# Moving the tiles of a gated attention-and-MLP kernel in SBUF: 512 bytes left unused low on the left, 2016 bytes at the top of the right

## The chip, the cores and the metric

The kernel runs on one core of a Trainium2 chip. The metric is the device time of one execution in microseconds (us); of a kernel that was run several times the median counts, and smaller is better. The core has five engines with a queue each: PE (TensorE, matrix products), ACT (ScalarE), DVE (VectorE), POOL (GpSimd) and SP (SyncE, which issues most DMAs). Tiles lie in SBUF, 128 partitions with the same layout of bytes in each; products land in PSUM, in banks of 512 float32 per partition. An address below is always the byte within a partition, since a tile starts at the same byte in all its partitions.

## The reference

Two branches over the same 2048 rows of x (512 columns) are mixed by a gate, one number for each row:

```python
def _A_ref(x, wqkv, wo):                 # attention, 32 heads of 16 columns
    H = 32; Dh = D // H
    q, k, v = ...                        # x @ wqkv, split in heads
    scores = jnp.einsum("bhqd,bhkd->bhqk", q, k) * Dh ** -0.5
    p = _softmax(scores, axis=-1)
    o = jnp.einsum("bhqk,bhkd->bhqd", p, v)
    return o (heads side by side) @ wo

def _B_ref(x, w1, w3, w2):               # gated MLP, inner width 1792
    h = _silu(x @ w1) * (x @ w3)
    return h @ w2

g = _sigmoid((x * gate_w).sum(-1, keepdims=True))
return g * a + (1 - g) * b
```

All inputs and the output are float32.

## The kernel before

**Products in three terms.** A float32 matrix product other than the attention's is made of three matmuls of type float32r: each operand is split into a high part and a low part (`xH`, `xL`; `fh`, `fl`), and high·high, high·low and low·high are added up in one PSUM bank. A matmul has two operands: the stationary one, up to 128 columns of 4 bytes (512 bytes of each partition), which a weight load (PEld in the profile) puts into the array first, and the moving one, here nearly always 512 columns (2048 bytes of each partition), which then streams through. In the profile's names `f<-xH,fh` the moving operand comes first and the stationary one second.

**Stages.** A prologue of some 85 us transposes x into `xH` and `xL`, computes Q and K of the first 8 heads (`project_qk`, L181) and all of V (`sums_v`, through `three`, L95 to L97). The main loop follows, written out by a string `order` of letters, and takes most of the time:

- `Q` (`score`, L719): the scores of two heads for 128 keys and 512 queries, two matmuls side by side on the upper and the lower half of the array's rows (stationary `Kt`, moving `Qt`, 50 rows each), into one of two PSUM tiles `S`; then ACT takes the exponential of it into one of ten tiles `p` (L723).
- `F` (`feed`): one matmul each of two other products, again side by side on the two halves of the rows (64 rows each). These products are the rest of Q and K and the MLP's two inner products (`w_product`, L409: stationary weights `fh`, `fl`, `raw`, `gw`; moving `xH`, `xL`), then h @ w2 (`h_product`, L518: stationary pieces of h in `fh`, `fl`, `raw`, `fr`, `gw`, `hx`; moving w2, which has taken the place of x in the tiles `xH`, `xL`), and part of the attention's last product (`o_product`, L597).
- `P` (`pv`, L706): the sums over keys p·V of two of the finished `p` tiles, in float32, four matmuls on four groups of the array's columns (stationary 17 columns of `V`, moving `p`).

A unit of the loop is eight `Q`. The first 83 units are

```python
one = "QFFF" * 7 + "QPPPP"
two = ["QFFF" * 5 + "QPPQQPP", "QFFF" * 6 + "PPQQPP"]
order = "QQFFF" + one * LONG + "".join(two[...] for i in range(short))
order += "QFFF" * 4 + "QPPQPP"
```

with LONG = 83, and with MID = 0 all of the 44 later units are `two[0]`. Counted out, the string has 2 + 127·8 + 6 = 1024 `Q` and 3 + 83·21 + 44·15 + 12 = 2418 `F`. PE executes this in the order of the string. A `Q` waits until ACT has emptied the `S` tile that was filled two `Q` earlier.

After the loop, `three` (L95 to L97) makes the last products with wo: for t = 6 and 7 with stationary pieces `ot` in `raw` and `gw`, and from t = 8 on with stationary `Oh`, `Ol`, which lie in `xH`, `xL` and `p`. The moving tiles are the same in both (`wo_`: parts of `xH3`, `xL3`, `p8`, `p9`).

**Where tiles lie.** SBUF is given out from two ends. Pools without a side stack up from low addresses: constants, then `xH`, `xL` (pool `xp`), `V` (`vp`), `Qt`, `Kt` (`qkp`), and in the loop the tiles `p` and `u` (`wk`). Pools with `side="right"` stack down from the top: `fw` (tags that begin with f: `fr`, `fh1`, `fl1`, `fh3`, `fl3`), `fk` (`gw`, `raw`, `sg`, `hx`, `gs`), and for the prologue `p1` (`xn`, `wh`, `wl`, `hi`, `lo`). In the loop the left side ended at byte 185856 and the right side began at 188384, with 2528 bytes between them. The built program gives these starts:

| tiles | side | bytes of one | start of the first | remainder by 2048 | by 512 | by 64 |
|---|---|---|---|---|---|---|
| `ident` | left | 512 | 16512 | 128 | 128 | 0 |
| `xH`, `xL` | left | 8192 | 17920 | 1536 | 0 | 0 |
| `V` | left | 34816 | 83456 | 1536 | 0 | 0 |
| `Qt` | left | 4096 | 118272 | 1536 | 0 | 0 |
| `Kt` | left | 8192 | 126464 | 1536 | 0 | 0 |
| `p`, `u` | left | 4096, 2048 | 142848 | 1536 | 0 | 0 |
| `xn`, `wh`, `wl`, `hi`, `lo` | right | 2048 to 8192 | 146016 | 608 | 96 | 32 |
| `gw`, `raw`, `sg`, `hx`, `gs`, `fr` | right | 2048 | 188384 | 2016 | 480 | 32 |
| `fh1`, `fl1`, `fh3`, `fl3` | right | 2048 | 212960 | 2016 | 480 | 32 |

Every tile of a row has the remainders of its row. A stationary slice of `xH`, `Kt`, `fh` or `raw` begins 512 bytes times a whole number behind the start of its tile, and a moving slice 2048 bytes times a whole number behind it, but for `V` in the products of L706, whose slices of 17 columns begin at any multiple of 4.

Of the kernel before, what the change touches and what calls it, by code (L numbers as in the profile page):

```python
# [8 lines left out]
F32 = mybir.dt.float32  # L9
# [8 lines left out]
P = 128  # L18
# [15 lines left out]
def gated_mix_kernel(ctx: ExitStack, tc: tile.TileContext, x, wqkv, wo, w1, w3, w2, gate_w, out):  # L34
# [20 lines left out]
    out = out[0]  # L55

    const = ctx.enter_context(tc.tile_pool(name="const", bufs=1))
    dram = ctx.enter_context(tc.tile_pool(name="dram", bufs=1, space=DRAM))
    psum = ctx.enter_context(tc.tile_pool(name="psum", bufs=1, space=PSUM))
    xp = ctx.enter_context(tc.tile_pool(name="xp", bufs=1))  # L60
    vp = ctx.enter_context(tc.tile_pool(name="vp", bufs=1))
    qkp = ctx.enter_context(tc.tile_pool(name="qkp", bufs=1))
    fw = ctx.enter_context(tc.tile_pool(name="fw", bufs=2, side="right"))
    fk = ctx.enter_context(tc.tile_pool(name="fk", bufs=2, side="right"))
    ph1 = ExitStack()
# [782 lines left out]
```

## Time and profile before

| what | value |
|---|---|
| median of three runs | 1423.19 us (1422.14 to 1423.74) |
| profiled execution, span | 1417.6 us |
| median of the runs less that span | 5.6 us |
| PE busy in the span | 1408.8 us, 99% |
| ACT busy | 1033.2 us, 73% |
| DVE, POOL busy | 449.4 us, 32%; 321.1 us, 23% |
| mean share of the DMA engines | 39.6% for the main queue |

The profile gives the span of one execution, from its first to its last instruction; the device time of the three runs is longer by 5.6 us at the median, for what lies around the span. In the timeline's rows each number in front is the start of the first instruction of a group in us, the second the time from there to the end of its last one, and "x2" the count. Ends of matmuls are modelled (one matmul overlaps the next), so the spacing of two starts says how long PE took, and the second number does not.

### The profile page before, as it was taken

To read this page: it belongs to the slowest core of one execution; us is meant where nothing else is said; L and a number is where in the kernel's file an instruction comes from. 1 tells how busy PE (TensorE), PEld (TensorE's weight loads), DVE (VectorE), ACT (ScalarE), POOL (GpSimd) and SP (SyncE) were. 2 spreads that over 40 slices of the span, in tenths; PEclk is the share of its full clock that TensorE was granted. 3 is DMA by queue.
4 is the path that set the end of the run, shared out by engine and by line. 5 is a ranking of instruction groups with operands and counts; after the bars stand their busy time and mean duration, and the time that the engine had idled before them with its cause. 6 is when DMAs were issued, how large, how long until landed. Compare 5 with 4: busy or idle time off the path is not lost.

```text
span 1417.6 us, 28518 instructions
## 1 busy us (share of the span) xinstructions
PE 1408.8 (99%) x11399; PEld 833.7 (59%) x11399; DVE 449.4 (32%) x845; ACT 1033.2 (73%) x1153; POOL 321.1 (23%) x356
## 2 busy tenths in 40 slices
PE   9999999999999999999999999999999999999998
PEld 7865656656556566565565665655555555554556
DVE  4421102464555545455464545400000000000013
ACT  4556767777777777777777777777788778877870
POOL 5014443011011100110110015441332332233230
PEclk9999999999999999999999999999999999999999
DMA  7554455342124432223233234543534443345445
GB/s 197 141 121 114 126 140 128 73 110 69 46 61 85 113 69 61 70 72 87 68 76 79 76 81 122 136 101 74 126 81 102 104 105 70 66 112 106 106 133 182
DMA packets 112668, 141.42 MB, mean 100 GB/s; under 512 B 16400, under 2 KB 70672, under 8 KB 109456
## 3 DMA queue, kind: packets, MB, share of 16 engines
q1 hardware_dynamic: 110384, 135.72, 39.6%
q10 hardware_dynamic: 2144, 3.80, 0.8%
q8 instruction: 92, 1.51, 0.5%
q14 instruction: 48, 0.39, 0.1%
HBM read 90.70 MB, written 48.76 MB: 98 GB/s over the span
## 4 chain that ended last, share of the span: by engine, by line
PE 93%; POOL 0%; DMA 0%; DVE 0%; ACT 0%; issue 0%; SPq 0%; ACTq 0%; POOLq 0%
PE acc L706 32%; PE f L409 27%; PE S L719 19%; PE f L518 11%; PE f L597 1%; PE f L95 0%; PE f L97 0%; PE f L96 0%; DMA fr<-in_B_w_dram 0%; PE S L97 0%; PE S L96 0%; PE S L95 0%; POOL xL L489 0%; POOL fl L489 0%; DVE sg L458 0%; POOL xH L488 0%
## 5 line engine op out<-in xcount | busy, mean ns | idle before, releaser
L723 ACT ACTIVATE p<-S 128x1024 f32<-128x1024 f32 x1024 | 967.5, 1026 | 308.4 <-PE S L719 307.1
L706 PE MATMUL acc<-p,V 128*17 128x512 f32 x4096 | 473.5, 594 | 0.0
L719 PE MATMUL S<-Qt,Kt 50*128 50x512 f32 x2048 | 427.9, 413 | 1.1 <-POOLq L278 0.6
L719 PEld LDWEIGHTS S<-Qt,Kt 50*128 50x128 f32 x2048 | 193.8, 184 | 187.4 <-ACT p L723 80.4
L706 PEld LDWEIGHTS acc<-p,V 128*17 128x17 f32 x4096 | 102.8, 97 | 274.1 <-issue 273.9
L409 PE MATMUL f<-xL,fh 64*128 64x512 f32 x1024 | 205.1, 391 | 0.0
L409 PE MATMUL f<-xH,fl 64*128 64x512 f32 x1024 | 204.9, 390 | 0.0
L409 PE MATMUL f<-xH,fh 64*128 64x512 f32 x1024 | 204.7, 390 | 0.0
L440 DVE RECIPROCAL sg<-sg 128x64 f32<-128x64 f32 x448 | 201.2, 509 | 1.9
L409 PEld LDWEIGHTS f<-xL,fh 64*128 64x128 f32 x1024 | 99.4, 187 | 21.2
L409 PEld LDWEIGHTS f<-xH,fl 64*128 64x128 f32 x1024 | 98.5, 185 | 20.1
L409 PEld LDWEIGHTS f<-xH,fh 64*128 64x128 f32 x1024 | 99.4, 187 | 17.7
L321 POOL CAST fh<-fr 128x512 fp32r<-128x512 f32 x32 | 21.6, 674 | 371.1 <-DMA fr<-in_B_w_dram 246.5
L687 DVE COPY u<-acc 128x512 f32<-128x512 f32 x32 | 22.1, 692 | 257.0 <-PE acc L706 257.0
L518 PE MATMUL f<-xH,fl 64*128 64x512 f32 x224 | 82.2, 391 | 0.5 <-POOL fl L489 0.5
L518 PE MATMUL f<-xL,fh 64*128 64x512 f32 x224 | 82.2, 391 | 0.3 <-POOL xL L489 0.3
L518 PE MATMUL f<-xH,fh 64*128 64x512 f32 x224 | 82.1, 391 | 0.0
L518 PE MATMUL f<-xH,raw 64*128 64x512 f32 x192 | 74.9, 390 | 0.0
L532 DVE TENSOR_SCALAR gs<-f,omg 128x512 f32<-128x512 f32 x16 | 12.0, 751 | 176.4 <-PE f L518 176.4
L432 DVE COPY gs<-f 128x512 f32<-128x512 f32 x56 | 38.7, 691 | 78.1 <-PE f L409 78.1
L518 PE MATMUL f<-xH,fr 64*128 64x512 f32 x160 | 62.4, 390 | 0.0
L454 DVE TENSOR_TENSOR raw<-f,gs 128x512 f32<-128x512 f32 x50 | 34.1, 682 | 82.7 <-PE f L409 82.7
(216 smaller groups left out, 1309.6 us busy)
## 6 DMA issues: line engine op xcount, KB each, us to landing
Kt<-kH_d SPq DMA_DIRECT2D x128, 128.0 KB
h_d<-sg SPq DMA_DIRECT2D x56, 256.0 KB
sg<-h_d SPq DMA_DIRECT2D x43, 256.0 KB
fr<-in_B_w_dram SPq DMA_DIRECT2D x42, 256.0 KB
Qt<-qH_d SPq DMA_DIRECT2D x128, 64.0 KB
Kt<-kL_d SPq DMA_DIRECT2D x64, 128.0 KB
fr<-in_A_wqkv_dram SPq DMA_DIRECT2D x18, 256.0 KB
Qt<-qL_d SPq DMA_DIRECT2D x64, 64.0 KB
```

What stands on the lines that cost most here:

```text
L321: nc.gpsimd.tensor_copy(wh, r)
L409: nc.tensor.matmul(ps, w[i == 2][r, k, :], (xL if i == 1 else xH)[b][r, k, :], start=n == 0 and r.start == 0, stop=n == 3 * ND - 1 and r.s ...
L432: nc.vector.tensor_copy(gs, ps)
L440: small.append(lambda q=q: nc.vector.reciprocal(sg[:, q:q + 64], sg[:, q:q + 64]))
L454: nc.vector.tensor_mul(gu, ps, st["gs"])
L518: nc.tensor.matmul(ps, hs[t][q][i == 2][r, P * o:P * o + P], (w2L if i == 1 else w2H)[q][r, o, :], start=n == 0 and r.start == 0, stop=n = ...
L532: nc.vector.tensor_scalar(y, ps, omg[:, t:t + 1], None, op0=OP.mult)
L597: nc.tensor.matmul(ps, ot[t][i == 2][r, P * k:P * k + P], wo_[k][i == 1][r, :], start=n == 0 and r.start == 0, stop=n == 3 * ND - 1 and r. ...
L687: nc.vector.tensor_copy(u, acc)
L706: nc.tensor.matmul(acc[r:r + DH + 1, :], V[:, k, 2 * j + h, :], p[:, h, :], start=k == 0, stop=k == NT - 1)
L719: nc.tensor.matmul(ps[:, h, :], Kt[i][r:r + 50, P * k:P * k + P], Qt[i][r:r + 50, t:t + 512], start=True, stop=True)
L723: nc.scalar.activation(p, ps, AF.Exp, scale=SCALE)
```

## The change

The change allocates two tiles that nothing writes or reads. `low_pad`, 128 float32 (512 bytes), comes right after the constants, so every left tile behind it starts 512 bytes higher. `top_pad`, 504 float32 (2016 bytes), is the first on the right, so every right tile starts 2016 bytes lower. The two together take the 2528 bytes that were free.

```diff
@@ -55,11 +55,15 @@
     const = ctx.enter_context(tc.tile_pool(name="const", bufs=1))
+    low_pad = ctx.enter_context(tc.tile_pool(name="low_pad", bufs=1))
+    low_pad.tile([P, 128], F32, name="low_pad")
     dram = ctx.enter_context(tc.tile_pool(name="dram", bufs=1, space=DRAM))
     psum = ctx.enter_context(tc.tile_pool(name="psum", bufs=1, space=PSUM))
     xp = ctx.enter_context(tc.tile_pool(name="xp", bufs=1))
     vp = ctx.enter_context(tc.tile_pool(name="vp", bufs=1))
     qkp = ctx.enter_context(tc.tile_pool(name="qkp", bufs=1))
+    top_pad = ctx.enter_context(tc.tile_pool(name="top_pad", bufs=1, side="right"))
+    top_pad.tile([P, 504], F32, name="top_pad")
     fw = ctx.enter_context(tc.tile_pool(name="fw", bufs=2, side="right"))
     fk = ctx.enter_context(tc.tile_pool(name="fk", bufs=2, side="right"))
```

The order of instructions on all five engines, and what each waits for, is the same in both built programs; only line numbers behind the change are higher by four. PSUM and DRAM addresses are the same. The starts become:

| tiles | start of the first, now | remainder by 2048 | by 512 | by 64 |
|---|---|---|---|---|
| constants with `ident` | unchanged | 128 (`ident`) | 128 | 0 |
| `xH`, `xL`, `V`, `Qt`, `Kt`, `p`, `u` | 18432 (`xH0`) | 0 | 0 | 0 |
| `xn`, `wh`, `wl`, `hi`, `lo` | 144000 | 640 | 128 | 0 |
| `gw`, `raw`, `sg`, `hx`, `gs`, `fr`, `fh`, `fl` | 186368 (`gw`) | 0 | 0 | 0 |

## The prediction

> **What bounds the kernel now.** I read the page first: busy shares, the clock, the chain of work that ended last, and the costliest groups.
>
> ```profile
> span 1417.6 us, 28518 instructions
> ...
> PE 1408.8 (99%) x11399; PEld 833.7 (59%) x11399; DVE 449.4 (32%) x845; ACT 1033.2 (73%) x1153; POOL 321.1 (23%) x356
> ...
> PEclk9999999999999999999999999999999999999999
> ...
> PE 93%; POOL 0%; DMA 0%; DVE 0%; ACT 0%; issue 0%; SPq 0%; ACTq 0%; POOLq 0%
> ...
> L723 ACT ACTIVATE p<-S 128x1024 f32<-128x1024 f32 x1024 | 967.5, 1026 | 308.4 <-PE S L719 307.1
> ...
> L409 PE MATMUL f<-xL,fh 64*128 64x512 f32 x1024 | 205.1, 391 | 0.0
> ```
>
> PE is busy 99% of the span at a granted clock near full speed, and 93% of the chain is PE's. No queue and no DMA ends a long wait, so what the change is worth is what it does to the spacing of matmuls. The change moves no instruction; only addresses differ. So the question is whether the trace shows a spacing that goes with an address. I therefore asked for PE's timeline in one unit of the main loop, with one row per letter of the order.
>
> ```profile
> 192.17 0.50 PE L719 MATMUL S<-Qt,Kt 50*128 50x512 f32 x2
> 192.51 0.40 PE L409 MATMUL f<-xH,fh 64*128 64x512 f32 x2
> ...
> 193.21 0.39 PE L719 MATMUL S<-Qt,Kt 50*128 50x512 f32 x2
> 193.45 0.39 PE L409 MATMUL f<-xH,fh 64*128 64x512 f32 x2
> 193.68 0.40 PE L409 MATMUL f<-xL,fh 64*128 64x512 f32 x2
> 193.91 0.40 PE L409 MATMUL f<-xH,fl 64*128 64x512 f32 x2
> 194.15 0.40 PE L719 MATMUL S<-Qt,Kt 50*128 50x512 f32 x2
> ...
> 198.78 0.39 PE L719 MATMUL S<-Qt,Kt 50*128 50x512 f32 x2
> 199.10 0.62 PE L706 MATMUL acc<-p,V 128*17 128x512 f32 x4
> ```
>
> From 193.21 to 198.78 six quartets QFFF take 5.57 us, 0.928 each, 0.232 per slot. No slot waits long. In all these slots the moving tile lies left, at a multiple of 512 bytes. The stationary one is `Kt` (left, multiple of 512) in a Q, and `fh` or `fl` (right, 32 bytes past a multiple of 64) in the three F.
>
> **Does a slot's time go with the address?** The products with wo after the loop answer that, since there the stationary tile goes from right to left while the moving tiles, the line of code and the shapes stay. At 1391.53 the stationary operand changes from `raw` and `gw` to `xH` and `xL`:
>
> ```profile
> 1386.17 0.39 PE L96 MATMUL f<-xL,raw 128*128 128x512 f32 x1
> ...
> 1390.83 0.39 PE L95 MATMUL f<-p,raw 128*128 128x512 f32 x1
> 1391.06 0.40 PE L96 MATMUL f<-p,raw 128*128 128x512 f32 x1
> 1391.30 0.39 PE L97 MATMUL f<-p,gw 128*128 128x512 f32 x1
> 1391.53 0.39 PE L95 MATMUL S<-xH,xH 128*128 128x512 f32 x1
> ...
> 1400.82 0.39 PE L97 MATMUL f<-xH,xL 128*128 128x512 f32 x1
> ...
> 1403.32 0.39 PE L96 MATMUL f<-p,xH 128*128 128x512 f32 x1
> ```
>
> From 1386.17 to 1391.53 there are 23 matmuls, 0.2330 each. From 1391.53 to 1403.32 there are 52, 0.2267 each. The difference is 0.0063 us, 2.7%. The output bank also changes, from `f` to `S`, but the rows from 1400.82 write `f` again and stay at 0.2267. Nor is it that the rest of the chip calms down. The busy times of both stretches (columns: PE, PEld, DVE, ACT, POOL, clock, DMA share, GB/s):
>
> ```profile
> 1386.00:1391.50 5.50, 5.50 (x24) 4.44 (x25) 1.06 (x3) 0.00 (x0) 0.00 (x0) 1.00 0.50 145
> 1391.50:1397.00 5.50, 5.50 (x26) 4.53 (x25) 1.38 (x3) 0.00 (x0) 0.00 (x0) 1.00 1.00 362
> ```
>
> The faster stretch has twice the DMA traffic and more DVE. The prologue gives two more cases: V with a right moving tile on a left stationary one, Q and K with a right stationary tile (`wh`, `wl`) lower in SBUF, at bytes that the left `p` tiles hold later.
>
> ```profile
> 83.62 0.40 PE L97 MATMUL f<-fh,xL 128*128 128x512 f32 x1
> ...
> 84.32 0.40 PE L97 MATMUL f<-fh,xL 128*128 128x512 f32 x1
> ...
> 40.00 1.09 PE L181 MATMUL S<-xH,wh 128*128 128x512 f32 x4
> ...
> 44.68 1.09 PE L181 MATMUL S<-xH,wl 128*128 128x512 f32 x4
> ```
>
> Three V matmuls take 0.70 us, 0.233 each; the twenty from 40.00 to 44.68 take 4.68, 0.234 each. So every case with one operand at 32 past a multiple of 64 stands at 0.233, wherever in SBUF it lies, and the one case with both on multiples of 512 at 0.2267. The quartet fits the same reading: one slot with both operands aligned and three with the stationary one off is 0.2267 + 3 × 0.2330 = 0.9257, against 0.928 measured. Four unaligned slots would be 0.932, four aligned ones 0.907.
>
> **The change part by part.** `top_pad` puts all the right tiles of the loop on multiples of 2048, and the prologue's on 640 past one, a multiple of 128. Whether the limit is 64, 128 or 512 bytes the trace doesn't tell; for the loop it doesn't matter. `low_pad` moves left tiles that already sit on multiples of 512. I price it at nothing: the slices of `Kt` begin at different multiples of 512 now, a new one every second Q, and the quartet shown (0.94) and the mean of six (0.928) differ by no more than the rows' rounding and the order within a pair allow.
>
> Price of an F slot. Directly, 0.2330 less 0.2267 is 0.0063. From the quartet, (0.928 − 0.907) / 3 is 0.0070. For single matmuls I take the first, for the loop the second, since it is measured there, 0.021 per quartet.
>
> Price of the P slots: none. Their moving `p` is aligned before and after, and the `V` slices stay at every multiple of 4.
>
> What limits the gain is ACT, since each quartet asks it for one exponential. The start of the loop shows ACT at its own rate, with a normal unit for comparison:
>
> ```profile
> 86.20 9.27 ACT L723 ACTIVATE p<-S 128x1024 f32<-128x1024 f32 x10 [7.85 <-PE S L719]
> ...
> 192.78 7.52 ACT L723 ACTIVATE p<-S 128x1024 f32<-128x1024 f32 x8 [2.96 <-PE S L719]
> ...
> 87.27 0.49 PE L719 MATMUL S<-Qt,Kt 50*128 50x512 f32 x2 [0.51 <-ACT p L723]
> ...
> 91.86 0.54 PE L719 MATMUL S<-Qt,Kt 50*128 50x512 f32 x2
> ...
> 88.03 1.95 ACT L723 ACTIVATE p<-S 128x1024 f32<-128x1024 f32 x2
> ...
> 90.03 0.53 PE L719 MATMUL S<-Qt,Kt 50*128 50x512 f32 x2
> ```
>
> There ACT works without a break, and PE, which waits for it, makes five quartets in 4.59 us: 0.918 each. That is what ACT sustains. Now it is asked every 0.928; after the change PE would ask every 0.907, faster than ACT can, and the backlog grows by 0.011 per quartet. The two `S` tiles give slack. In a unit the last Q starts at 198.78 and the last exponential ends at 192.78 + 7.52 = 200.30, so a tile is free 1.52 us after its Q began. The weight load of the Q that reuses it comes two quartets later less one slot: 1.814 − 0.227 = 1.587 after the change. The signal takes 0.05: in the stretch that ACT holds, the exponential that ends at 88.03 + 1.95 = 89.98 lets the Q of 90.03 go. That leaves 0.017. The unit's second Q comes 0.11 late, behind the P (192.17 to 193.21 is 1.04), so the backlog starts with the third exponential, and with the fourth it is 0.022. The Q that waits for the fourth is the sixth. So four of the unit's quartets go at 0.907 and the rest at ACT's 0.918.
>
> The sum, by places:
> - 83 long units with seven quartets: four at −0.021 and three at −0.010 are −0.114 each, −9.5 us.
> - 44 short units with five quartets: four at −0.021 and one at −0.010 are −0.094 each, −4.1 us.
> - The loop's first 3 and last 12 F, five quartets: −0.1 us.
> - The prologue has 96 matmuls of L181 and 192 with a right moving tile: 288 × 0.0063 = 1.8 us. PE has gaps there which take part of it. I take −1.0, between 0 and −1.8.
> - The 24 matmuls after the loop: −0.2 us.
>
> Together −14.9 us. The span of 1417.6 becomes 1402.7, and with the 5.6 us around it 1408.3, against the median of 1423.2. If ACT never holds PE, units give −0.147 and −0.105, with the rest −18.1: 1405.1. If it holds PE from the first quartet on, −0.070 and −0.050, with the rest −9.3: 1413.9.
>
> The P part of a unit covers what ACT still owes: its 2.96 us of idle time in the row above lie there. The one long stall in the loop is this step of the chain:
>
> ```profile
> 912.42 4.25 DMA fr<-in_B_w_dram
> ```
>
> It starts from work of PE that ends just before, and moves with it. DVE, POOL and the DMAs have idle time all along and only start earlier.
>
> **The rivals.**
> - *ACT is the bound at once* (1414). For it: 0.918 against 0.907. Against it: the slack of the two `S` tiles that I worked out. Chance 0.13.
> - *The address is not the cause* (1422 to 1423). All F slots in the trace are pairs on two halves of the rows, and no aligned pair with F's shapes is there; their 0.232 could be the price of the pair. Then only single matmuls gain, 1.2 us by the sum above, or nothing. Against it: the quartet fits one aligned and three unaligned slots within 0.002. Chance 0.11. [...]
> - *Equal offsets collide* (slower). With all large tiles on multiples of 2048, PE's two reads and the writes of ACT, POOL and DMA start at the same offset by 2048, where left and right are 480 bytes apart now. If that cost a slot what the odd start costs, 0.0063, the 2418 F would add 15.2 us: 1438.4. It decides from a mean quartet of 0.928 on. Against it: the fastest stretch, 1391.53 to 1403.32, has moving and stationary tiles at the same offset by 2048 (1536) in a quarter of its matmuls, and these are no slower in the rows, and twice the DMA traffic. Chance 0.07.
> - *More than forecast* (1403): ACT never holds PE, and Q slots, too, lose time that an F's load costs them now. A further 0.0023 per quartet (0.928 less 0.9257) would be 1.8 us over 801 quartets: 1403.3. Chance 0.05.
>
> **How the numbers follow.** The forecast, a gain of 11 to 18 us with some hold by ACT, has 0.64; the others are as above. The predicted time is 1408. The range 1403 to 1420 holds the forecast, ACT's rival and part of the last one, and leaves out the two that end at or over today's time, with 0.18 between them. A change under 0.2% (2.8 us) can hardly be told from none here. Faster by more: 0.64 + 0.13 + 0.05 = 0.82. Within it: 0.11. Slower: 0.07.
>
> **What would show it.** In the profile after, the quartet should stand near 0.907 in a unit's first half and near 0.918 at its end, the matmuls around `raw` and `gw` after the loop at 0.2267 like those behind them, V at 0.2267, and ACT's idle time before L723 (308.4 us) shorter by about what the loop gains. A quartet still at 0.928 with single matmuls at 0.2267 would mean that pairs have their own price. Quartets of 0.918 throughout would mean that ACT holds from the start. V at 0.2267 but L181 at 0.234 would say that 128 bytes are not enough. I am wrong altogether if the tail's two speeds come from something else than where a tile starts.

## The result: no gain, at most a quarter of a per cent slower

The changed kernel takes 1424.31 us (median of 22 runs, 1419.98 to 1427.12) against 1422.22 of the kernel before (22 runs, 1417.92 to 1423.74): a ratio of 1.0014, with an interval of 1.0004 to 1.0024. Predicted was 1408, with a range of 1403 to 1420. The runs of both kernels fall into two groups some 4 to 5 us apart (medians 1418.8 and 1423.2 before, 1420.4 and 1425.7 after), with about half of the runs in each, and within each group the changed kernel is the slower one, by 1.7 and by 2.5 us.

The page of the profile after, to be read against the rows of before:

```profile
span 1422.6 us, 28518 instructions
...
PE 1413.5 (99%) x11399; PEld 837.8 (59%) x11399; DVE 448.3 (32%) x845; ACT 1036.5 (73%) x1153; POOL 321.5 (23%) x356
...
PEclk9989999999999999999999999999999999999999
```

Nothing has changed in kind: PE is still busy 99%. The third digit of the clock is an 8, which was a 9. The windows of the same trace around that place (columns: length, then busy time and count of PE, PEld, DVE, ACT and POOL, then clock, DMA share and GB/s):

```profile
84.00:88.00 4.00, 3.50 (x18) 2.50 (x17) 0.00 (x0) 3.55 (x4) 0.00 (x0) 0.82 0.43 135
88.00:92.00 4.00, 4.00 (x14) 3.10 (x12) 0.00 (x0) 2.33 (x3) 0.00 (x0) 0.50 1.03 135
92.00:96.00 4.00, 4.00 (x20) 3.00 (x20) 0.00 (x0) 2.26 (x3) 0.00 (x0) 0.50 0.27 33
96.00:100.00 4.00, 4.00 (x33) 1.47 (x34) 0.00 (x0) 1.84 (x2) 0.00 (x0) 0.90 0.02 4
```

The granted clock is 0.50 from 88 to 96 us, at the start of the loop, where before's profile has 1.00. The profiled execution, 1424.69 us, is one of the upper group and has a mean granted clock of 0.996. Over a whole execution of after that mean is 0.995 to 0.996 in every run of the upper group and 0.999 to 1.000 in every run of the lower one. So the two profiled spans, after's with this dip of the clock and before's without, can't be set side by side. The trace of the kernel with the right shift alone (`top_only`, below) has no such dip (1.00 from 84 to 96 us) and a span of 1417.6 us, 5.0 less than after's. Most of the 5.0 is the dip: the unit of the loop in which it lies takes 15.15 us in after and 10.53 in `top_only`. So `top_only` is the kernel to set beside before's profile.

**The places that the prediction named.** The timeline of PE after, first at the end of the prologue (V, and the loop's first Q), then in the products with wo after the loop:

```profile
78.67 0.39 PE L101 MATMUL f<-fh,xL 128*128 128x512 f32 x1
...
82.07 0.39 PE L101 MATMUL f<-fh,xL 128*128 128x512 f32 x1
...
83.59 0.93 PE L723 MATMUL S<-Qt,Kt 50*128 50x512 f32 x4 [1.14 <-SPq L282]
```

```profile
1393.57 0.39 PE L101 MATMUL f<-p,raw 128*128 128x512 f32 x1
...
1396.51 0.39 PE L99 MATMUL S<-xH,xH 128*128 128x512 f32 x1
```

V's fifteen steps from 78.67 to 82.07 are 0.2267 each, where they were 0.233. Of the 23 with stationary `raw` and `gw`, which took 0.2330 each, the last thirteen, from 1393.57 to 1396.51, take 0.227 each; the ten ahead of them, from 1391.25 on, still take 0.231. So single matmuls did what was forecast, those behind the loop only after ten steps. Now a unit of the loop:

```profile
617.73 0.40 PE L723 MATMUL S<-Qt,Kt 50*128 50x512 f32 x2
617.96 0.40 PE L413 MATMUL f<-xH,fh 64*128 64x512 f32 x2
618.20 0.40 PE L413 MATMUL f<-xL,fh 64*128 64x512 f32 x2
618.43 0.39 PE L413 MATMUL f<-xH,fl 64*128 64x512 f32 x2
618.66 0.40 PE L723 MATMUL S<-Qt,Kt 50*128 50x512 f32 x2
...
623.33 0.39 PE L723 MATMUL S<-Qt,Kt 50*128 50x512 f32 x2
```

Six quartets QFFF take 5.60 us, 0.933 each. They took 0.928. The quartet, which should have gone to 0.907, got longer by 0.005.

**Where the time went.** The first Q and the first product with wo bound the loop. Their rows before, and then with the right shift alone:

```profile
85.33 0.93 PE L719 MATMUL S<-Qt,Kt 50*128 50x512 f32 x4 [0.61 <-POOLq L278]
...
1385.83 0.51 PE L95 MATMUL f<-xH,raw 128*128 128x512 f32 x1
```

```profile
83.67 0.93 PE L721 MATMUL S<-Qt,Kt 50*128 50x512 f32 x4 [1.20 <-SPq L280]
...
1385.89 0.50 PE L97 MATMUL f<-xH,raw 128*128 128x512 f32 x1
```

The prologue is 1.66 us shorter (85.33 to 83.67). The loop is 1.72 longer: 1385.83 − 85.33 = 1300.50 against 1385.89 − 83.67 = 1302.22. A long unit, from its first Q to the next unit's, takes 10.495 us before and 10.520 here (medians of the 83 units in the timelines). One of them, near 917 us, is no measure of the change: in before PE waits 0.28 and 0.49 us there for POOL's `xL` and `fl`, in `top_only` it doesn't, and the unit takes 11.81 and 10.80. The other 82 add 2.3 us and the 44 short ones 0.4. So the loop is 2.7 us longer apart from that wait and the prologue 1.7 shorter, which leaves 1.1, near the 1.7 that the runs show.

### The profile page after: what moved, and what is told of

It is laid out like the page before. It is cut to its first block, busy times and chain, and to the rows that moved or that the text cites. A ratio compares the mean times of both kernels' runs of the same rounds, so it can differ in the third digit from the quotient of the medians.

```text
span 1422.6 us, 28518 instructions
## 1 busy us (share of the span) xinstructions
PE 1413.5 (99%) x11399; PEld 837.8 (59%) x11399; DVE 448.3 (32%) x845; ACT 1036.5 (73%) x1153; POOL 321.5 (23%) x356
## 4 chain that ended last, share of the span: by engine, by line
PE 92%; DMA 1%; POOL 1%; issue 0%; SPq 0%; ACT 0%; DVE 0%; ACTq 0%; POOLq 0%
PE acc L710 32%; PE f L413 27%; PE S L723 19%; PE f L522 11%; PE f L601 1%; DMA fr<-in_B_w_dram 1%; POOL xL L493 0%; DMA Kt<-kH_d 0%; PE f L99 0%; PE f L100 0%; PE f L101 0%; PE S L100 0%; PE S L99 0%; PE S L101 0%; DMA fr<-h_d 0%; POOL fl L493 0%
## 5 line engine op out<-in xcount | busy, mean ns | idle before, releaser
L723 PEld LDWEIGHTS S<-Qt,Kt 50*128 50x128 f32 x2048 | 197.6, 185 | 187.8 <-ACT p L727 80.0
L413 PE MATMUL f<-xH,fh 64*128 64x512 f32 x1024 | 207.7, 396 | 0.0
L522 PE MATMUL f<-xH,fh 64*128 64x512 f32 x224 | 83.0, 395 | 0.0
```

The lines of the kernel that those rows point to most:

```text
L413: nc.tensor.matmul(ps, w[i == 2][r, k, :], (xL if i == 1 else xH)[b][r, k, :], start=n == 0 and r.start == 0, stop=n == 3 * ND - 1 and r.s ...
L522: nc.tensor.matmul(ps, hs[t][q][i == 2][r, P * o:P * o + P], (w2L if i == 1 else w2H)[q][r, o, :], start=n == 0 and r.start == 0, stop=n = ...
L723: nc.tensor.matmul(ps[:, h, :], Kt[i][r:r + 50, P * k:P * k + P], Qt[i][r:r + 50, t:t + 512], start=True, stop=True)
```

## The experiments

### One part of the change alone

Three kernels: the left shift alone (`low_only`), the right one alone (`top_only`), and the right one with 992 bytes (`top_992`), where left and right tiles are 512 apart by 2048.

```diff
 low_only:
+    low_pad = ctx.enter_context(tc.tile_pool(name="low_pad", bufs=1))
+    low_pad.tile([P, 128], F32, name="low_pad")
 top_only, and with 248 in place of 504 top_992:
+    top_pad = ctx.enter_context(tc.tile_pool(name="top_pad", bufs=1, side="right"))
+    top_pad.tile([P, 504], F32, name="top_pad")
```

> Only the 512 bytes on the left are left unused: left tiles at 0, right tiles still at 2016 past a multiple of 2048. If the pair has its own price: within 2 us of before, quartet between 0.927 and 0.934. If it is the left shift that made the loop's quartet go from 0.927 to 0.933: 3 to 5 us slower than before, since the prologue gains nothing. If equal offsets of left and right collide: as before, quartet 0.927, since the offsets still differ (by 32 bytes).

> Only the 2016 bytes on the right are left unused: left tiles at 1536, right tiles at 0 past a multiple of 2048, all on multiples of 512. If the pair has its own price: quartet 0.927 to 0.934, time within 3 us of before. If the left shift is at fault, or if equal offsets collide: quartet 0.907 to 0.918, 8 to 15 us faster than before.

> 992 bytes on the right are left unused and none on the left: left tiles at 1536, right tiles at 1024 past a multiple of 2048. Same forecast as for 2016 bytes on the right alone: a pair with its own price gives 0.927 to 0.934 per quartet; a collision of equal offsets, by 2048, gives 0.907 to 0.918; a collision of offsets equal by 1024 or 512 gives what the changed kernel has, 0.933.

Measured: `low_only` 1422.95 us, ratio 1.0004 (0.9988 to 1.0020), quartet 0.928. `top_only` 1424.60, ratio 1.0015 (1.0001 to 1.0029), quartet 0.933. `top_992` 1424.08, ratio 1.0013 (0.9998 to 1.0027), quartet 0.933. (These ratios, and those further below, are to runs of the kernel before that were made along with each of these kernels.) The left shift does nothing, the right one does all that the change does, and that left and right begin at the same offset by 2048 plays no part, since they are 512 apart in `top_only` and `top_992`. A collision of offsets that are equal by 512 would also give 0.933 in all three kernels, so these runs don't exclude it; `m1` and `q64_after` below do.

### Addresses by themselves (m1 and m3)

`m1` leaves the computation out. It has two tiles, `M` (moving) and `W` (stationary), and blocks of 48 equal matmuls, each block with its own byte offsets; its comments name them in bytes ("s" for singles, "w" for the stationary operand, "m" for the moving one). After them come pairs and quartets. One of the blocks:

```diff
+    for n in range(N):  # s w32 m0
+        nc.tensor.matmul(f[0], W[:, 8 + 128 * (n % 8):8 + 128 * (n % 8) + 128],
+                         M[:, 0 + 512 * (n % 4):0 + 512 * (n % 4) + 512], start=n == 0, stop=n == N - 1)
```

> This kernel leaves the whole computation out: it runs blocks of 48 products on one core with nothing beside them, single matmuls (128 rows) and pairs on the two halves of the rows (64 rows each), with the stationary (w) or the moving operand (m) at 0, 4, 16, 32 or 64 bytes past a multiple of 2048, and then quartets of one Q pair and three F pairs with and without an ACT exponential. Theory 'each operand off a multiple of 64 costs 0.0066 us, pairs too': singles and pairs 0.2267 at 0 and 64, 0.2333 at 32; quartets 0.907 with all at 0, 0.927 with the F weights at 32. Rival 'a pair has its own price': singles 0.2267 and 0.2333 as above, but pairs 0.232 to 0.2335 whatever the address, and quartets 0.927 to 0.934 in both. Rival 'equal offsets collide': pairs at 0 with 0 slower than pairs at 0 with 64, quartets at 0 without ACT as slow as in the loop (0.933).

The timeline has one row per block of singles. Stationary and moving offsets are, in order: 0 and 0, 32 and 0, 0 and 32, 32 and 32, 64 and 0, 16 and 0, 4 and 0:

```profile
8.05 11.15 PE L64 MATMUL f<-M,W 128*128 128x512 f32 x48
19.04 11.36 PE L67 MATMUL f<-M,W 128*128 128x512 f32 x48
30.23 11.36 PE L70 MATMUL f<-M,W 128*128 128x512 f32 x48
41.43 11.08 PE L73 MATMUL f<-M,W 128*128 128x512 f32 x48
52.35 11.36 PE L76 MATMUL f<-M,W 128*128 128x512 f32 x48
63.55 11.36 PE L79 MATMUL f<-M,W 128*128 128x512 f32 x48
74.74 11.31 PE L82 MATMUL f<-M,W 128*128 128x512 f32 x48
```

Start to start over 48, the blocks with one operand shifted stand at 0.2333 (30.23 to 41.43), also at 64 (52.35 to 63.55). The one with both at 32 is faster: 41.43 to 52.35 is 0.2275, and 0.2267 once seven or so steps have passed. So it isn't that each operand wants a multiple of 64; two equally odd starts are as good as two even ones. Pairs of 64 rows gave the same: 0.2267, 0.2333, 0.2333, 0.2267 for these first four. The rival that pairs have a price of their own is refuted too, and so is a collision of equal offsets, since those take 0.2267. The two halves of a pair keep a pace of their own: with the upper half's stationary operand at 0 and the lower half's at 32, the upper half takes 0.2267 per step and the lower one 0.2333.

In the same kernel quartets with a Q of 50 rows took 0.9266 with all offsets at 0 and 0.9267 with F's stationary at 32. Here the stationary operand's address was worth nothing, and in the kernel no gain either. ACT working alongside on 384 columns left the settled quartets at that (0.9267 in both). With F's moving operand at 32 instead they settled at 0.933.

`m3` asks pairs for 33 combinations of offsets, 32 pairs each.

> The computation is left out. Blocks of 32 pairs (64 rows each) with the stationary operand (w) and the moving one (m) at so many bytes past a multiple of 512 (moving: of 2048). Theory 'what counts is the difference of the two offsets': 0.2267 where w equals m (0 and 0, 32 and 32, 64 and 64, 128 and 128, 256 and 256), 0.2333 in most others, also where both are multiples of 64. Rival 'each operand has to begin on a multiple of 64 (or 128, or 256)': 0.2267 in every case where both do, and at 32 and 32 not.

The timeline of `m3` at three blocks' starts and the starts of the blocks that follow them: stationary at 32 (L76), at 256 (L104), both at 32 (L164):

```profile
30.39 0.39 PE L76 MATMUL f<-M,W 64*128 64x512 f32 x1
...
37.85 0.39 PE L80 MATMUL f<-M,W 64*128 64x512 f32 x1
...
82.50 0.39 PE L104 MATMUL f<-M,W 64*128 64x512 f32 x1
...
89.77 0.40 PE L108 MATMUL f<-M,W 64*128 64x512 f32 x1
...
193.48 0.39 PE L164 MATMUL f<-M,W 64*128 64x512 f32 x1
...
200.75 0.39 PE L168 MATMUL f<-M,W 64*128 64x512 f32 x1
```

Over 32 pairs these are 0.2331, 0.2272 and 0.2272 each. The settled steps of all blocks (means from the ninth pair on), in us:

| offsets (stationary, moving), bytes | step |
|---|---|
| difference 0 or 256: (0,0), (256,0), (0,256), (32,32), (64,64), (128,128), (256,256) | 0.2267 to 0.2271 |
| (192,0), (448,0), (0,64) | 0.2287 to 0.2289 |
| (4,0), (16,0), (32,0), (48,0), (64,0), (96,0), (128,0), (160,0), (320,0), (384,0), (480,0) | 0.2322 to 0.2343 |
| (0,16), (0,32), (0,128), (0,192), (0,384), (0,448), (0,480) | 0.2316 to 0.2335 |
| (96,32), (160,32), (480,448), (128,64) | 0.2327 to 0.2334 |
| (496,0) | 0.2267 |

Apart from the last row, which I can't explain (its difference, 240 by 256, is that of the slow (0,16) as well), the steps of 0.227 are those whose offsets differ by a multiple of 256. The second row has a common difference too: stationary less moving is 192 in all three, counted by 256. Why these stand in between is open. The multiple of 256 covers the kernel's own cases as well: before, the right side was 480 from the left (0.233), after it is 0 (0.2267), and L185, the prologue's products with `wh`, at 640, which is 128 by 256, did not gain (rows of after):

```profile
41.28 1.10 PE L185 MATMUL S<-xH,wh 128*128 128x512 f32 x4
...
44.08 0.39 PE L99 MATMUL f<-fh,xH 128*128 128x512 f32 x1
```

Those 12 steps take 2.80 us, 0.2333 each.

So in these blocks the step depends, by 3% (0.2267 against 0.2333), on where the two operands lie relative to each other; what makes it so, no run here shows. Starts 16, 32 or 64 apart all take longer than equal ones, by the table from 0.2287 to 0.2343.

### Quartets: what holds the loop (m2)

The quartet was indifferent to the address of F's stationary operand, so something else in it costs the time that an address costs a lone matmul. `m2`, again without the computation, varies it: the rows of Q, Q's bank, the offsets, the count of F. Two of its blocks differ in this:

```diff
-            nc.tensor.matmul(ps[:, 0, :], W[0:50, ...], M[0:50, ...], start=True, stop=True)
+            nc.tensor.matmul(ps[:, 0, :], W[0:64, ...], M[0:64, ...], start=True, stop=True)
```

> The computation is left out. Blocks of 16 quartets, one pair Q and three (or four) pairs F, no ACT, all operands on multiples of 512 bytes unless the name says otherwise (w32, m32: F's operand 32 bytes on; all32: Q's too). K50, K48, K32, K64 is the number of rows of Q; S, f, g the PSUM banks of Q (two alternating tiles as in the kernel; F's own; two fixed others); low1: the lower half runs one step ahead of the upper. Theory 'the rows break the pace': Q with 64 rows gives 0.907 per quartet, with 50, 48 or 32 rows 0.920 to 0.933, in whatever bank. Rival 'the bank breaks it': 0.907 only where Q writes F's banks. Rival 'any change of addresses from a steady walk breaks it': no quartet at 0.907. Singles with another bank every 4 or every matmul: 0.2267 if the bank doesn't matter.

Timeline of `m2`, Q on the upper half: the block with 50 rows (second to sixteenth Q), that with 64 rows (first to ninth), and the one in which Q and F alike have 50 rows (second to sixteenth):

```profile
9.56 0.39 PE L65 MATMUL S<-M,W 50*128 50x512 f32 x1
...
22.63 0.39 PE L65 MATMUL S<-M,W 50*128 50x512 f32 x1
...
23.56 0.39 PE L73 MATMUL S<-M,W 64*128 64x512 f32 x1
...
30.82 0.39 PE L73 MATMUL S<-M,W 64*128 64x512 f32 x1
...
97.88 0.39 PE L109 MATMUL S<-M,W 50*128 50x512 f32 x1
...
110.58 0.39 PE L109 MATMUL S<-M,W 50*128 50x512 f32 x1
```

14 quartets in 13.07 us are 0.9336, 8 in 7.26 are 0.9075, and 14 in 12.70 are 0.9071. All operands are at offset 0 in the three. The rest: with Q writing another bank 0.907 (64 rows) and 0.933 (50 rows); with 48 rows 0.933; with 32 rows 1.318, for which no run shows the reason; with the lower half one step ahead 0.907 (64 rows) and 0.933 (50 rows). So neither the bank nor 50 rows cost anything, but a change of rows from one slot to the next does, 0.027 us per quartet here. With four F the quintet takes 1.133 (64 rows) and 1.160 (50 rows), again 0.027 more.

With 64 rows throughout, an address counts in the quartet as well: 0.936 with F's stationary at 32, 0.927 with its moving tile there too, 0.907 with all at 32. In the second of these each slot's own two operands are 0 apart, in Q and in F, and yet it is slow. So an equal difference within each slot isn't enough in a mix: here the neighbours' offsets had to agree as well.

### The kernel with Q on 64 rows (q64_after, q64_before, q64_224)

If that is right, the addresses can pay as soon as Q has 64 rows. `Kt` and `Qt` have room: rows 50 to 63 of each half are free. Zeros in `Qt` there add nothing to the sums.

```diff
+        zero = slot("sg", F32)
+        nc.gpsimd.memset(zero, 0.0)
+        for i in range(2):
+            for r in (32, 96):
+                for j in range(2):
+                    nc.gpsimd.tensor_copy(Qt[i][r:r + 32, 512 * j:512 * j + 512], zero[r:r + 32, :])
...
-            nc.tensor.matmul(ps[:, h, :], Kt[i][r:r + 50, P * k:P * k + P],
-                             Qt[i][r:r + 50, t:t + 512], start=True, stop=True)
+            nc.tensor.matmul(ps[:, h, :], Kt[i][r:r + 64, P * k:P * k + P],
+                             Qt[i][r:r + 64, t:t + 512], start=True, stop=True)
```

`q64_after` adds this to the changed kernel, `q64_before` to the kernel before, `q64_224` to the kernel before with only 224 bytes unused on the right, where right and left differ by 256. The quartets in the table are medians over 82 long units of each trace.

> The changed kernel, with Q's two matmuls on 64 rows each in place of 50 (rows 50 to 63 of the Qt tiles are set to zero once, so the sums stay). Theory 'a change in the number of rows from one slot to the next takes the aligned addresses' gain away': quartet 0.907 in a unit's first half, held by ACT at about 0.918 towards its end, 11 to 18 us faster than before. Rival 'the loop's other work (ACT's writes, DMA) breaks the pace too': quartet 0.927 to 0.934, within 3 us of before.

> The kernel before, with Q on 64 rows and the old addresses (stationary F operands 480 bytes off the moving ones, by 512). If the difference of the offsets counts, the quartet is 0.936 as in the block of quartets with 64 rows and the weights 32 bytes on, and the time 5 to 9 us longer than before. If rows alone count: 0.907 to 0.918, 8 to 18 us shorter.

> Q on 64 rows, nothing unused on the left, 224 bytes on the right: left tiles at 1536, right ones at 1792 past a multiple of 2048, so 256 apart. If a difference of a multiple of 256 is enough: the same time as with 64 rows and the change, within 2 us (Q and K of the prologue, 128 apart, gain nothing, 0.6 us). If it needs 512 or 2048: quartet 0.927 to 0.936, no gain.

| kernel | rows of Q | right less left, by 512 | median us | ratio to before | quartets 2 to 7 of long units |
|---|---|---|---|---|---|
| before | 50 | 480 | 1422.22 | 1 | 0.925 to 0.928 |
| after | 50 | 0 | 1424.31 | 1.0014 (1.0004 to 1.0024) | 0.933 |
| q64_before | 64 | 480 | 1417.69 | 0.9983 (0.9969 to 0.9997) | 0.927 |
| q64_after | 64 | 0 | 1406.22 | 0.9901 (0.9881 to 0.9921) | 0.907 to 0.926 |
| q64_224 | 64 | 256 | 1406.65 | 0.9909 (0.9890 to 0.9928) | 0.907 to 0.919 |

The row count alone brings 0.2% in the ratio, the address alone nothing, both together 1%: whichever of the two is left as it was keeps the slots at their slow pace. Part of that is that a mean granted clock of 0.996 was rarer in the runs of the three new kernels (3 of 12, 1 of 6 and 2 of 6, in the table's order, against 8 of 17 of before beside them); without those runs the medians are 1419.0 us for before, then 1417.6, 1406.2 and 1406.4, so 0.1% for the rows alone and 0.9% for both. That 224 bytes do as well as 2016 confirms the 256. `q64_before` missed its expected quartet (0.936, from `m2`), since it stands at 0.927, and its time, which was to be 5 to 9 us longer and is 1.4 shorter. The timeline of PE in a unit of `q64_before`, Q rows alone, from the second Q to the eighth:

```profile
623.05 0.39 PE L725 MATMUL S<-Qt,Kt 64*128 64x512 f32 x2
...
628.61 0.40 PE L725 MATMUL S<-Qt,Kt 64*128 64x512 f32 x2
```

Six quartets take 5.56 us, 0.927 each. And in a unit of `q64_after`:

```profile
617.41 0.50 PE L729 MATMUL S<-Qt,Kt 64*128 64x512 f32 x2
...
618.44 0.39 PE L729 MATMUL S<-Qt,Kt 64*128 64x512 f32 x2
...
619.34 0.40 PE L729 MATMUL S<-Qt,Kt 64*128 64x512 f32 x2
...
622.07 0.40 PE L729 MATMUL S<-Qt,Kt 64*128 64x512 f32 x2
...
622.99 0.45 PE L729 MATMUL S<-Qt,Kt 64*128 64x512 f32 x2
...
623.90 0.46 PE L729 MATMUL S<-Qt,Kt 64*128 64x512 f32 x2
```

From 618.44 to 622.07 four quartets take 3.63 us, 0.907 each. The last two take 0.92 and 0.91. Over 82 long units the medians are 0.912 and 0.926 for the sixth and seventh, 0.907 for the third to fifth and 0.917 for the second. The end of the unit is where the prediction had ACT hold PE.

### Is it ACT? (act480)

`q64_after` with exponentials and sums p·V over 480 of the 512 queries; the last 32 of each 512 are left out:

```diff
-                nc.tensor.matmul(acc[r:r + DH + 1, :], V[:, k, 2 * j + h, :], p[:, h, :],
+                nc.tensor.matmul(acc[r:r + DH + 1, 0:480], V[:, k, 2 * j + h, :], p[:, h, 0:480],
...
-        nc.scalar.activation(p, ps, AF.Exp, scale=SCALE)
+        nc.scalar.activation(p[:, :, 0:480], ps[:, :, 0:480], AF.Exp, scale=SCALE)
```

> As with 64 rows and the change, but the exponential and the product p V work on 480 of each 512 queries (the rest is left out), so ACT needs about 0.06 us less per exponential. If it is ACT that holds the later quartets of a unit: all of them at 0.907, the sixth and seventh too, where they stood at 0.912 and 0.917 to 0.927. If something else holds them, they stay. The total says nothing here, since the P slots shrink as well.

```profile
595.58 0.40 PE L729 MATMUL S<-Qt,Kt 64*128 64x512 f32 x2
...
600.13 0.39 PE L729 MATMUL S<-Qt,Kt 64*128 64x512 f32 x2
601.03 0.39 PE L729 MATMUL S<-Qt,Kt 64*128 64x512 f32 x2
```

The unit in this timeline of PE runs at 0.908 from 595.58 to 601.03 (six quartets, 5.45 us), and its last quartet takes 0.90. The medians of the sixth and seventh are 0.907. With less work for ACT (972 ns for an exponential at the mean, 1033 in `q64_after`) the late quartets run like those in the middle, so ACT it was. The second quartet stays at 0.917, so that one isn't ACT's. The total, 1375.91, also has shorter P slots and isn't compared.

### Why 0.928 became 0.933 (m4)

With rows mixed, `m1` had shown 0.9266 and `m2` 0.9336 for the same addresses. `m4`, without the computation, repeats quartets, each block behind another lead of small matmuls, with F's stationary at 0 and at 480 (the addresses of after and of before). One of the leads, with the first line of its block:

```diff
+    for _ in range(2):
+        nc.tensor.matmul(f[2][:, 0:92], W[:, 0:128], M[:, 0:92], start=True, stop=True)
...
+    for n in range(16):  # q K50 w0 lead1
```

> The computation is left out. Blocks of 16 quartets, with Q on 50 or on 64 rows and the F weights at 0 or at 480 bytes past a multiple of 512 (all else on multiples of 512), each behind a few matmuls of another length, so that every block begins at another phase. The question is why quartets with 50 rows and equal offsets took 0.9267 in one set of blocks, 0.9333 in another and 0.933 in the changed kernel, and 0.927 to 0.928 in the kernel before. If the addresses alone set the pace: one value for each kind in all blocks (50 rows and 0: 0.9333; 50 rows and 480: 0.927). If the phase at the start sets it too: both values appear within one kind. With 64 rows and 0 all blocks settle at 0.9067.

Timeline of `m4`, Q on the upper half, second to sixteenth Q: a block with 480 (L79), then one with 0 (L112):

```profile
24.23 0.39 PE L79 MATMUL S<-M,W 50*128 50x512 f32 x1
...
37.20 0.39 PE L79 MATMUL S<-M,W 50*128 50x512 f32 x1
...
70.62 0.39 PE L112 MATMUL S<-M,W 50*128 50x512 f32 x1
...
83.69 0.39 PE L112 MATMUL S<-M,W 50*128 50x512 f32 x1
```

14 quartets take 12.97 us (0.926) with 480 and 13.07 (0.934) with 0. With 50 rows all eight blocks at 480 stand at 0.926 to 0.928 on both halves. At 0 the upper half stands at 0.933 in all eight, the lower one at 0.926 or 0.927 in two and at 0.932 to 0.934 in six. With 64 rows it turns round: 0.907 to 0.908 in four of four at 0, 0.933 at 480 (one half of one block 0.927). So the kernel's small loss is reproduced without the kernel: under mixed rows the equal addresses are a little worse than the odd ones. That the step also depends on how a block begins is seen in the two lower halves; `m1` and `m2` differ in that too, but they also ran on different chips. What selects it, and why a change of rows costs anything, stays open.

## Why the prediction was wrong, by its steps

- **The reading of the quartet** failed: "one slot with both operands aligned and three with the stationary one off is 0.2267 + 3 × 0.2330 = 0.9257, against 0.928 measured". The sum fits by chance. A quartet of Q on 50 rows among F on 64 takes 0.926 to 0.934 whatever F's address is (`m1`, `m2`, `m4`), as the change of rows keeps the slots from the fast pace; with 50 rows throughout or 64 throughout it is 0.907 (`m2`). The columns "50*128 50x512" and "64*128 64x512" stood in the quoted rows, and I weighed the address only.
- **The price of F**, 0.0070 each and 0.021 per quartet, rested on that reading and on "four aligned ones 0.907". In place of the 0.021 that it was to save, a quartet became 0.005 longer. With it fall the terms for long units (−9.5), short units (−4.1) and the ends of the loop (−0.1): the loop of `top_only` is 1.7 us longer than before's, not 13.7 shorter. The 0.907 holds for 64 rows throughout, and there the sum's size is near: `q64_after` less `q64_before` is −11.5 us, where the whole sum was −14.9.
- **"Every case with one operand at 32 past a multiple of 64"** named the wrong quantity. In the uniform streams of `m1` and `m3` what counted is how far the two operands differ, counted by 256 bytes: 0.2267 to 0.2271 in `m3` where the difference is a multiple of that, 0.2287 to 0.2343 in the other blocks but one. For the tail and V both readings give the same. The prediction's sign for 128 bytes not being enough came true: V at 0.2267, L185 at 0.2333.
- **Prologue and tail** were right in kind: V went to 0.2267, the products around `raw` after ten of them, and in `top_only`'s trace the prologue is 1.7 us shorter, against 1.0 forecast, without a gain of L185.
- **The left shift**, priced at nothing, cost nothing (`low_only`, 1.0004).
- **ACT's hold** from the sixth quartet on was right as a mechanism, and could not show in after because PE never got to 0.907. In `q64_after` it does: the sixth and seventh quartets take 0.912 and 0.926, and 0.907 in `act480`.
- **The 5.6 us around the span** were mostly something else. In the profiled execution of after the time is 1424.69 us for a span of 1422.6: 2.1 us. The other 3.5 came from setting the span of an execution without the dip against the median of three runs of the upper group.
- **The rivals.** "The address is not the cause" came nearest in time (1422 to 1423), but its reason, a price of the pair, is refuted by `m1`; the loop kept its pace because of the rows. So the sign "A quartet still at 0.928 with single matmuls at 0.2267" came about, nearly (0.933), and meant something else than the prediction said. Equal offsets do not collide: in `m1` they give the 0.2267, and `q64_after`, where the loop's tiles of both sides begin on multiples of 2048, is, with `q64_224`, the fastest of the whole kernels.

## What to carry to other kernels

A pace read from one mix of instructions may have two causes, each of which alone keeps it slow; before an address or any other cause is priced there, look for a second difference within the mix, shapes first, and measure the mix without it. For streams of 512-column float32r matmuls like these, try starts of all stationary and moving tiles of neighbouring slots that differ by multiples of 256 bytes (`m3`: 0.2267 to 0.2271 a step, against 0.2287 to 0.2343 in 25 of the 26 other blocks) together with the same number of rows in neighbouring slots, padded with zeros where needed (`m2`: 0.907 a quartet, against 0.933): in this kernel both together brought 0.9 to 1.0%, one alone 0.1 to 0.2% or nothing.

## What the hardware showed unexpectedly

- Most settled means lie on one grid: 0.2267, 0.2333, 0.9067, 0.9267 and 0.9333 us are 34, 35, 136, 139 and 140 times 6.67 ns, the difference of the first two. It isn't a rule for all: 0.2289 and 0.936 lie off it, and in slow blocks single steps vary (0.228 to 0.241 in `m3` with the stationary operand at 128).
- Mixing 50 and 64 rows costs 0.020 or 0.027 us per quartet (0.9266 in `m1`, 0.9336 in `m2`, against 0.907), though 50 rows throughout cost none (0.907 in `m2`, as with 64). Whether it is the weight load that a change of rows delays, no run shows.
- With 32 rows in Q the quartet took 1.318.
- The clock of 0.50 at the loop's start, for some 10 us by the windows of after's trace, is in the traces of after and `top_992` and not in those of before and `top_only`; `low_only`'s trace has a dip of 3.4 us at 922.6 instead. In after's trace it follows a PE wait of 1.14 us, but `top_only` has a wait of 1.20 at the same place and no dip. It cost 4.6 us in after's first long unit, more than anything that the change did.
